# Spreading the softmax reciprocals over 64 partitions: PE transposes against a trip through DRAM

## Chip, cores and metric

The kernel runs on one core of a Trainium2 chip. The metric is the device time of one execution in microseconds (us); lower is better. Before the change the median of three runs was 1174.25 us (1172.53 to 1176.54).

## What is computed

Attention with a memory term, for 4 batches, 8 heads, 576 positions and 64 values a head, followed by two gated feed-forward layers (MoE and MoE2, 2304 rows, width 512, inner width 1536), all in fp32:

```python
scores = scale * np.matmul(q, k.transpose(0, 1, 3, 2))      # causal mask
a = np.exp(scores - scores.max(-1, keepdims=True))
a /= a.sum(-1, keepdims=True) + 1e-09
local = np.matmul(a, v)
mem_out = mem_ret / mem_norm                                # q_p M_prev and q_p z_prev
attn = g * mem_out + (1 - g) * local                        # g = sigmoid(beta)
x = attn as [2304, 512]
x = (sigmoid(x @ w_gate) * (x @ w_val)) @ w_out             # MoE
out = ((x @ w_a) * (x @ w_b)) @ w_out2                      # MoE2
```

## The kernel before, in words

Attention works on 16 pairs (a batch and two of its heads; `p` counts them, 4 pairs make a batch). Rows of a pair lie in five blocks: X_ (blocks 0, 2, 3) and Y_ (blocks 1, 4). In pass `p` of the main loop the scores and exponentials of pair `p` are made, and what is left of pair `p - 1` (`old`) is finished:

- `scores` (L195): q times k in fp32 for both heads into two large PSUM tiles `sc`. `expo` (L224 on DVE, L229 on ACT): minimum, exponential and row sums `sm`.
- `turn_w` (L311): transposes of the exponentials on PE through the identity matrix, into PSUM tiles `tp`, and an evacuation (`aw`, L149 on ACT or L147 on DVE). There are three `tp` buffers (a fourth for the first pairs), and every transpose, every evacuation and every product with v takes one.
- `sums(old)`: the memory norm and the row sums, with the gate folded in, become `t` [128 x 10], one value for each row, block and head; L290 takes its reciprocal on DVE. L292 on POOL copies each value to 64 columns, `rt` [128 x 5 x 2 x 64].
- `turn_r(old, X_)` and `turn_r(old, Y_)`: five transposes of `rt` on PE (L341) into two `tp` tiles and two copies on ACT (L346) into `x` [128 x 576]: now each of a head's 64 partitions holds the reciprocals of all rows.
- `pv(old, ...)`: products with M_prev (L360) and with v (L366), accumulated in a `tp` tile; L372 on DVE multiplies it with `x`, in place, and L376 stores `x` to DRAM.
- Between these the work for the first feed-forward layer is laid in: `M()` issues one group of three matmuls (L471 to L473, written `m<-xs,w` or `m<-gh,w`) at a time, `fill` issues steps of the weight preparation (loads `st`, L388 and L390; DVE L398 to L417; ACT; POOL), and `split_a` turns finished `x` tiles into pairs `xs`. `room(old)` makes sure that the `x` tile of four pairs ago has been split, since there are four of them.

All DMAs are issued by SP, in one order. A scheduler sets the order of each engine's instructions from the order of the program and from its own estimates; PE, DVE, ACT, POOL and SP then each run their list in that order. After the 16 pairs come the rest of the first layer and the second layer (matmuls `gv` and `mo`), which the change does not touch.

Of the kernel before, what the change touches and what calls it, by code (L numbers as in the profile page):

```python
# [9 lines left out]
F32 = mybir.dt.float32  # L10
F32R = mybir.dt.float32r
AF = mybir.ActivationFunctionType
# [7 lines left out]
def kernel(  # L20
# [16 lines left out]
    nc = tc.nc  # L37
    P = 128
    B, H, S, D = q.shape
    NPAIR = H // 2  # L40
# [5 lines left out]
    NB = 5  # L46
    ZX = 320
# [7 lines left out]
    vec, act, pool, pe = nc.vector, nc.scalar, nc.gpsimd, nc.tensor  # L55

    const = ctx.enter_context(tc.tile_pool(name="const", bufs=1))
    dram = ctx.enter_context(tc.tile_pool(name="dram", bufs=1, space=bass.MemoryType.DRAM))
# [6 lines left out]
    xp = lctx.enter_context(tc.tile_pool(name="xp", bufs=4))  # L65
    work = lctx.enter_context(tc.tile_pool(name="work", bufs=2))
    at = rctx.enter_context(tc.tile_pool(name="at", bufs=2, side="right"))
# [8 lines left out]
    H2 = (0, 1)  # L76
# [4 lines left out]
    def rows(i):  # L81
        return P if i else 64

    ident = const.tile([P, P], F32, name="ident")
# [4 lines left out]
    scs = [psa.tile([P, 1024], F32, tag=f"sc{e}", name="sc") for e in H2]  # L89
    sms = [at.tile([P, NB, 2], F32, name=f"sm{i}", bufs=1) for i in H2]  # L90
    xd = [dram.tile([P, NPAIR, S], F32, name=f"xd{i}") for i in range(B)]
    xb = {}
    st = {}

    X_, Y_ = (0, 2, 3), (1, 4)
    AT = {0: 0, 2: 64, 3: 192, 1: 320, 4: 448}
# [3 lines left out]
    def place(p):  # L100
        b, r = divmod(p, NPAIR)
        return b, 2 * r
# [48 lines left out]
    def tp():  # L151

        turns[0] += 1
        return (psx if psm is None and turns[0] % 4 == 0 else pst).tile([P, 512], F32, tag="tp", name="tp")
# [113 lines left out]
    def sums(p):  # L268

        _, h = place(p)
        t = at.tile([P, NB, 2], F32, tag="t", name="t")
        vec.scalar_tensor_tensor(
            out=t, in0=sms[p % 2], scalar=1e-9,
            in1=og[:, h:h + 2].rearrange("p (o h) -> p o h", o=1).to_broadcast([P, NB, 2]),
            op0=ALU.add, op1=ALU.mult,
        )
        nr = st.pop(("nr", p))  # L280
        vec.tensor_tensor(out=nr, in0=nr, in1=t, op=ALU.mult)
        qp = st.pop(("qp", p))
        for a in (slice(0, 3), slice(3, NB)):
            w = a.stop - a.start
            pool.tensor_tensor(
                out=mix(p)[:, a, :, 0:64], in0=qp[:, a],
                in1=nr[:, a].rearrange("p i (h o) -> p i h o", o=1).to_broadcast([P, w, 2, D]),
                op=ALU.mult,
            )
        vec.reciprocal(out=t, in_=t)  # L290
        rt = at.tile([P, NB, 2, D], F32, tag="rt", name="rt", bufs=1)
        pool.tensor_copy(  # L292
            out=rt, in_=t.rearrange("p i (h o) -> p i h o", o=1).to_broadcast([P, NB, 2, D])
        )
        st["rt", p] = rt


    PA = [(2, 1, 0), (3, 1, P), (2, 2, 2 * P), (3, 2, 3 * P)]
# [17 lines left out]
    def turn_mix(p, name):  # L316
# [11 lines left out]
        a = evac("am" + "XY"[name == "Y"], t, c, 1 if name == "Y" else 2, name in EDVE)  # L328
        for m, e in enumerate(es):
            st["m", p, e, blocks] = a[:, m * c // len(es):(m + 1) * c // len(es)]  # L330

    def turn_r(p, blocks):

        b, pr = divmod(p, NPAIR)
        if blocks is X_:
            xb[b, pr] = xp.tile([P, S], F32, tag="x", name="x")
        t0, w = (0, ZX) if blocks is X_ else (ZX, S - ZX)
        r = tp()
        for i in blocks:
            m, c = rows(i), AT[i] - t0  # L340
            pe.transpose(  # L341
                out=r[:, c:c + m],
                in_=st["rt", p][0:m, i].rearrange("p h d -> p (h d)"),
                identity=ident[0:m, 0:m],
            )
        act.activation(out=xb[b, pr][:, t0:t0 + w], in_=r[:, 0:w], func=AF.Copy)  # L346

    def pv(p, blocks):

# [360 lines left out]
    if True:  # L710
        start()
        wst = w_stream(
            [(w1, 0, c, kind, wp) for kind in range(3) for c in range(MA)]
            + [(w1, 0, c, kind, wp if c < KA else None) for c in range(MA, NCH) for kind in range(3)],
            2,
        )
        left = [1 + 9 * KA]

        def w_next():

            if left[0]:
                left[0] -= 1
                next(wst)

        batches = list(range(B - 1))
        cur, deferred, finished, cut_a = [], [], [], []
        split_q = []

        def settle():
            while deferred:  # L730
                deferred.pop(0)()

        def M():

            settle()
            if not cur:
                if not batches:
                    return False
                cur.append(moe_a(batches.pop(0)))
                cur.append(next(cur[0]))  # L740
            b, key, f, after = cur[1]
            if b not in cut_a or key not in ws:
                return False
            with tc.issue_after(st["anchor"].ins):
                f()
            if after:
                deferred.append(after)
            nx = next(cur[0], None)
            if nx is None:
                cur.clear()  # L750
            else:
                cur[1] = nx
            return True

        def Ms(k=1):
            for _ in range(k):
                M()

        def split(k):
            while k and split_q and split_q[0][0] <= done[0] and split_q[0][3] <= len(finished):  # L760
                _, f, a, _ = split_q.pop(0)
                f(*a)
                if a[-1] == KD - 1:
                    cut_a.append(a[0])
                k -= 1

        def fill(p):
            settle()
            split(1)
            if p >= 1:  # L770
                with tc.issue_after(st["pace"].ins):
                    for _ in range(1 if p < 4 else 2):
                        w_next()

        def room(p):

            old = divmod(p - 4, NPAIR)
            while any(x[1] is split_a and x[2] == old for x in split_q):
                split(1)
                if not M():  # L780
                    w_next()

        for b in range(B - 1):
            for kk in range(KD):
                split_q.append((NPAIR * b + kk + 1, split_a, (b, kk), b))
        for kk in range(KD):
            split_q.append((NPAIR * (B - 1) + kk + 1, split_last, (kk,), B - 1))

        load_q(0)
        load_k(0)  # L790
        load_z(0)
        load_v(0)
        for key in "kq":
            turn(0, key)
        turn4(0)
        for p in range(NP + 1):
            new = p < NP
            nx = p + 1 if p + 1 < NP else None
            old = p - 1 if p else None
            if p == NPAIR:  # L800
                pctx.close()
                mctx = ExitStack()
                psm = mctx.enter_context(
                    tc.tile_pool(name="psm", bufs=1, space=bass.MemoryType.PSUM, side="right")
                )

            if nx:
                load_q(nx)
                load_k(nx)
            if new:  # L810
                scores(p, X_)
                expo(p, X_)
            if old is not None:
                for e in H2:
                    turn_w(old, e, "B")
            Ms()
            if old is not None:
                for e in H2:
                    turn_w(old, e, "C")
                sums(old)  # L820
            Ms(2)
            fill(p)
            if new:
                phi1(p)
                if p:
                    load_v(p)
            if nx:
                load_z(nx)
                for key in "kq":
                    turn(nx, key)  # L830
            Ms(2)
            fill(p)

            if new:
                scores(p, Y_)
                expo(p, Y_)
            Ms()
            if old is not None:
                for name in "01Y":
                    turn_mix(old, name)  # L840
            Ms()
            if nx:
                turn4(nx)
            fill(p)
            if new:
                for e in H2:
                    turn_w(p, e, "A")
                phi2(p)
            Ms(2)
            if old is not None:  # L850
                room(old)
                turn_r(old, X_)
                turn_r(old, Y_)
                Ms()
                pv(old, X_)
                pv(old, Y_)
            Ms(2)
            fill(p)
        while cur or batches or split_q or deferred:
            M()  # L860
            fill(NP)
        while left[0]:
            w_next()
# [100 lines left out]
```

## Time and profile before

| | |
|---|---|
| median of 3 runs | 1174.25 us |
| the profiled execution, its own time | 1178.19 us |
| its span, first to last instruction | 1176.4 us (1.8 us lie around it) |
| PE busy | 1138.2 us (97%), mean granted clock 0.984 |
| weight loads of PE | 900.8 us (77%) |
| DVE busy | 542.1 us (46%) |
| ACT busy | 454.6 us (39%) |
| POOL busy | 285.1 us (24%) |
| DMA queue of SP | 24.1% of 16 engines |
| chain that ended last | PE 85%, DVE 7%, ACT 4%, others 4% |

The attention part ends near 369 us of the span; the rest is the feed-forward layers. The shares are means over stages with different limits, so a change in the attention part is read from its own stretch. The granted clock is a share of the full TensorE clock (2.4 GHz); 0.5 is its lower level (1.2 GHz).

### The profile page before, as it was taken

Reading aid. Unit: us, or ns where it says so; the run is one execution under the profiler, and the core shown is the slowest. Engines: PE = TensorE matmul, PEld = TensorE weight load, DVE = VectorE, ACT = ScalarE, POOL = GpSimd, SP = SyncE. Lnnn points to the kernel's source line nnn. Section 1 sums busy time; section 2 is a strip of 40 time slices with the busy share of each in tenths; the row PEclk is TensorE's granted clock in tenths of the full one; section 3 lists DMA queues with packets and bytes.
Section 4 is the critical chain, followed back from the end, with each engine's and each line's share of the span. In section 5 each row is a group of like instructions: output and inputs, shape, how many; then the busy total and the mean of one; then the engine's idle time right before and its main releaser. Section 6 shows DMA issues by size and latency. Waiting matters only on the chain.

```text
span 1176.4 us, 15633 instructions
## 1 busy us (share of the span) xinstructions
PE 1138.2 (97%) x5928; PEld 900.8 (77%) x5928; DVE 542.1 (46%) x1169; ACT 454.6 (39%) x977; POOL 285.1 (24%) x298
## 2 busy tenths in 40 slices
PE   6889889999999999999999999999999999999998
PEld 4555557667677888998788888888888888888897
DVE  5897875554544997127821388861100200200111
ACT  5777655765744444133411243432111211211221
POOL 2675563242230112111111111111111111111111
PEclk9898989999999999999999999999999999999999
DMA  6444434123002434013330334421000200100000
GB/s 155 107 124 123 118 83 122 47 70 105 25 22 98 133 112 135 37 55 126 118 115 1 107 111 159 125 72 36 36 1 1 72 1 1 59 1 1 5 36 19
DMA packets 109563, 84.39 MB, mean 72 GB/s; under 512 B 69168, under 2 KB 96816, under 8 KB 108592
## 3 DMA queue, kind: packets, MB, share of 16 engines
q1 hardware_dynamic: 109488, 83.39, 24.1%
q8 instruction: 47, 0.77, 0.3%
q14 instruction: 28, 0.23, 0.1%
HBM read 66.06 MB, written 17.30 MB: 71 GB/s over the span
## 4 chain that ended last, share of the span: by engine, by line
PE 85%; DVE 7%; ACT 4%; issue 1%; DMA 1%; POOL 1%; SPq 1%; POOLq 0%; DVEq 0%; ACTq 0%
PE gv L472 15%; PE gv L473 15%; PE gv L471 15%; PE mo L670 4%; PE mo L669 4%; PE mo L668 4%; PE mo L471 3%; PE mo L472 3%; PE mo L473 3%; PE sc L195 3%; PE m L471 3%; PE tp L366 3%; PE m L472 2%; PE m L473 2%; PE tp L311 2%; ACT s L229 2%
## 5 line engine op out<-in xcount | busy, mean ns | idle before, releaser
L471 PE MATMUL gv<-xs,w 128*128 128x512 f32 (+1 forms) x864 | 319.3, 370 | 1.3 <-ACT xs L623 1.3
L472 PE MATMUL gv<-xs,w 128*128 128x512 f32 (+1 forms) x864 | 319.2, 369 | 0.4 <-DVE xs L624 0.2
L473 PE MATMUL gv<-xs,w 128*128 128x512 f32 (+1 forms) x864 | 318.9, 369 | 0.0
L558 POOL TENSOR_TENSOR gl<-sg,gh 128x512 fp32r<-128x512 f32 (+1 forms) x120 | 144.8, 1207 | 698.6 <-ACT gh L149 698.6
L552 DVE TENSOR_TENSOR sg<-gv,sg 128x512 f32<-128x512 f32 (+1 forms) x108 | 68.2, 631 | 419.3 <-PE gv L473 414.9
L471 PEld LDWEIGHTS gv<-xs,w 128*128 128x128 f32 x864 | 163.1, 189 | 30.9 <-ACT xs L623 1.5
L472 PEld LDWEIGHTS gv<-xs,w 128*128 128x128 f32 x864 | 163.2, 189 | 30.6 <-DVE xs L616 0.8
L473 PEld LDWEIGHTS gv<-xs,w 128*128 128x128 f32 x864 | 163.2, 189 | 28.9
L149 ACT ACTIVATE gh<-sg 128x512 fp32r<-128x512 f32 (+1 forms) x120 | 70.6, 589 | 221.5 <-DVE sg L552 221.2
L638 ACT ACTIVATE sg<-gv 128x512 f32<-128x512 f32 (+1 forms) x108 | 59.1, 547 | 218.6 <-PE gv L473 216.5
L670 PE MATMUL mo<-w,gl 128*128 128x512 f32 x216 | 85.0, 394 | 0.1
L669 PE MATMUL mo<-w,gh 128*128 128x512 f32 x216 | 84.8, 393 | 0.0
L668 PE MATMUL mo<-w,gh 128*128 128x512 f32 x216 | 84.8, 392 | 0.0
L229 ACT ACTIVATE s<-s,mx 128x320 f32<-128x320 f32 (+3 forms) x128 | 77.5, 608 | 11.9 <-DVE mx L224 11.9
L149 ACT ACTIVATE aw<-tp 128x512 f32<-128x512 f32 (+2 forms) x112 | 56.0, 514 | 53.0 <-PE tp L311 32.8
L399 ACT ACTIVATE wt<-wt,rebias 128x512 int32<-128x512 int32 x72 | 51.8, 720 | 59.1 <-DVE wt L398 58.9
L224 DVE CUSTOM_DVE_ANT_0 s<-sc,mask 64x64 f32<-64x64 f32 (+4 forms) x160 | 69.0, 480 | 10.2 <-PE sc L195 7.8
L471 PE MATMUL mo<-gh,w 128*128 128x512 f32 (+1 forms) x192 | 70.2, 366 | 0.0
L472 PE MATMUL mo<-gl,w 128*128 128x512 f32 (+1 forms) x192 | 70.2, 366 | 0.0
L473 PE MATMUL mo<-gh,w 128*128 128x512 f32 (+1 forms) x192 | 70.2, 366 | 0.0
L195 PE MATMUL sc<-kt,qt 64*128 64x320 f32 (+4 forms) x384 | 63.1, 443 | 0.6 <-DVE mx L224 0.3
L436 ACT ACTIVATE w<-wt 128x512 fp32r<-128x512 f32 x57 | 36.0, 631 | 41.3 <-DVE wt L433 40.5
(102 smaller groups left out, 1593.7 us busy)
## 6 DMA issues: line engine op xcount, KB each, us to landing
st<-in_moe_w_out_dram SPq DMA_DIRECT2D x24, 512.0 KB, 3.5
st<-in_moe_w_gate_dram SPq DMA_DIRECT2D x12, 512.0 KB, 3.6
st<-in_moe_w_val_dram SPq DMA_DIRECT2D x12, 512.0 KB, 3.6
st<-in_moe_w_a_dram SPq DMA_DIRECT2D x12, 512.0 KB, 3.6
st<-in_moe_w_b_dram SPq DMA_DIRECT2D x12, 512.0 KB, 3.7
xd<-x SPq DMA_DIRECT2D x16, 288.0 KB, 2.8
qn<-in_q_dram SPq DMA_DIRECT2D x32, 128.0 KB, 3.0
kn<-in_k_dram SPq DMA_DIRECT2D x32, 128.0 KB, 3.1
```

Source lines behind the costliest of these rows:

```text
L149: act.activation(out=out, in_=src, func=AF.Copy)
L195: st["anchor"] = pe.matmul(scs[e][0:m, SC0[i] + a:SC0[i] + z], lhsT=st["q", p][r, r0:r0 + m], rhs=st["k", p][r, a:z], start=True, stop=True,)
L224: st["pace"] = vec.tensor_tensor_reduce(out=s, in0=scs[e][0:m, SC0[i]:SC0[i] + w], in1=mask[0:m, c:c + w], scale=1.0, scalar=BIG, op0=ALU. ...
L229: act.activation(out=o, in_=s, func=AF.Exp, scale=-1.0, bias=mx[0:m, i:i + 1], accum_out=sms[p % 2][0:m, i:i + 1, e],)
L471: pe.matmul(o, lhsT=w[:, 0, ws_], rhs=xh, start=first, stop=False, skip_group_check=True)
L472: pe.matmul(o, lhsT=w[:, 0, ws_], rhs=xl, start=False, stop=False, skip_group_check=True)
L473: pe.matmul(o, lhsT=w[:, 1, ws_], rhs=xh, start=False, stop=last, skip_group_check=True)
L552: st["gate"] = vec.tensor_tensor(out=s[:, 0:n], in0=vps[:, 0:n], in1=s[:, 0:n], op=ALU.mult)
L558: pool.tensor_tensor(out=gl[:, 0:n], in0=s[:, 0:n], in1=gh[:, 0:n].bitcast(F32), op=ALU.subtract)
L668: pe.matmul(mo[f], lhsT=gh[:, t], rhs=w[:, 0], start=first, stop=False)
L669: pe.matmul(mo[f], lhsT=gh[:, t], rhs=w[:, 1], start=False, stop=False)
L670: pe.matmul(mo[f], lhsT=gl[:, t], rhs=w[:, 0], start=False, stop=c == NCH - 1)
```

## The change

`rt`, its copy on POOL and `turn_r` are gone. In their place `spread(old)` transposes `t` [128 x 10] once on PE (L301 of the new file) into a `tp` tile [10 x 128], ACT copies it to `tt` (L305), SP stores it in five pieces of two rows each to a DRAM tile `rd` [2 x 576] (L310; one of four in turn), and SP loads each row of `rd` back into 64 partitions of `x` (L315, two transfers of 64 x 576). `spread` and the call of `room` stand right behind `sums(old)`, early in the pass, where `turn_r` stood near its end.

```diff
+    rds = [dram.tile([2, S], F32, name=f"rd{i}") for i in range(4)]
...
         vec.reciprocal(out=t, in_=t)
-        rt = at.tile([P, NB, 2, D], F32, tag="rt", name="rt", bufs=1)
-        pool.tensor_copy(
-            out=rt, in_=t.rearrange("p i (h o) -> p i h o", o=1).to_broadcast([P, NB, 2, D])
-        )
-        st["rt", p] = rt
+        st["t", p] = t
+
+    def spread(p):
...
+        b, pr = divmod(p, NPAIR)
+        r = tp()
+        pe.transpose(
+            out=r[0:2 * NB, 0:P], in_=st.pop(("t", p)).rearrange("p i h -> p (i h)"), identity=ident
+        )
+        tt = at.tile([2 * NB, P], F32, tag="tt", name="tt")
+        act.activation(out=tt, in_=r[0:2 * NB, 0:P], func=AF.Copy)
+        rd = rds[p % 4]
+        for i, k in ((0, 1), (1, 1), (2, 2), (4, 1)):
+            for m in range(k):
+                w = rows(i + m)
+                nc.sync.dma_start(
+                    out=rd[:, AT[i + m]:AT[i + m] + w], in_=tt[2 * (i + m):2 * (i + m) + 2, 0:w]
+                )
+        x = xb[b, pr] = xp.tile([P, S], F32, tag="x", name="x")
+        for e in H2:
+            nc.sync.dma_start(out=x[64 * e:64 * e + 64], in_=rd[e:e + 1].broadcast_to([64, S]))
...
-    def turn_r(p, blocks):
-
-        b, pr = divmod(p, NPAIR)
-        if blocks is X_:
-            xb[b, pr] = xp.tile([P, S], F32, tag="x", name="x")
-        t0, w = (0, ZX) if blocks is X_ else (ZX, S - ZX)
-        r = tp()
-        for i in blocks:
-            m, c = rows(i), AT[i] - t0
-            pe.transpose(
-                out=r[:, c:c + m],
-                in_=st["rt", p][0:m, i].rearrange("p h d -> p (h d)"),
-                identity=ident[0:m, 0:m],
-            )
-        act.activation(out=xb[b, pr][:, t0:t0 + w], in_=r[:, 0:w], func=AF.Copy)
...
                 sums(old)
+                room(old)
+                spread(old)
...
             if old is not None:
-                room(old)
-                turn_r(old, X_)
-                turn_r(old, Y_)
                 Ms()
                 pv(old, X_)
                 pv(old, Y_)
```

The scheduler makes a new order from it. Three places of it follow; line numbers of the new file are 1 to 20 off those of the old one (numbers behind names tell buffers apart; L331 is the old L311, L364 the old L360, L370 the old L366, L475 to L477 the old L471 to L473, L196 the old L195, L171 the old L170, L380 the old L376, L108 and L112 the old L107 and L111).

PE, pair 8, from its transposes `tp<-ident,s` to its products with v, before:

```order
L311 MATMUL tp_2364<-ident_87,s_2214 128x128 x4
L473 MATMUL m_2305<-xs_2192,w0_566 128x512
L341 MATMUL tp_2384<-ident_87,rt_2264 128x64
L341 MATMUL tp_2384<-ident_87,rt_2264 128x128 x2
L341 MATMUL tp_2389<-ident_87,rt_2264 128x128 x2
L471 MATMUL m_2379<-xs_1932,w0_743 128x512
L472 MATMUL m_2379<-xs_1932,w0_743 128x512
L473 MATMUL m_2379<-xs_1932,w0_743 128x512
L471 MATMUL m_2379<-xs_2020,w0_743 128x512
L472 MATMUL m_2379<-xs_2020,w0_743 128x512
L473 MATMUL m_2379<-xs_2020,w0_743 128x512
L360 MATMUL tp_2396<-aw_2334,mv_2040 64x320
```

The same place now:

```order
L331 MATMUL tp_2378<-ident_87,s_2218 128x128 x4
L475 MATMUL m_2393<-xs_2084,w0_757 128x512
L476 MATMUL m_2393<-xs_2084,w0_757 128x512
L477 MATMUL m_2393<-xs_2084,w0_757 128x512
L475 MATMUL m_2393<-xs_2196,w0_757 128x512
L476 MATMUL m_2393<-xs_2196,w0_757 128x512
L477 MATMUL m_2393<-xs_2196,w0_757 128x512
L364 MATMUL tp_2400<-aw_2348,mv_2054 64x320
L364 MATMUL tp_2400<-aw_2354,mv_2054 64x320
L370 MATMUL tp_2400<-aw_2140,vn_2053 64x256
```

The three rows of `rt` (five transposes) are gone from between the transposes `tp<-ident,s` and the products; six matmuls of the first layer still stand between.

PE, the same pass, about half a pass earlier, at the scores of the Y_ blocks, now:

```order
L196 MATMUL sc_92<-kt_2066,qt_2073 128x192
L196 MATMUL sc_93<-kt_2066,qt_2073 128x320
L196 MATMUL sc_92<-kt_2066,qt_2073 128x320
L196 MATMUL sc_93<-kt_2066,qt_2073 128x256
L301 MATMUL tp_2268<-ident_87,t_2262 10x128
L196 MATMUL sc_92<-kt_2066,qt_2073 128x256
L171 MATMUL tp_2300<-ident_87,kn_2203 128x128 x4
L171 MATMUL tp_2307<-ident_87,qn_2199 128x128 x4
L475 MATMUL m_2319<-xs_1936,w0_580 128x512
L476 MATMUL m_2319<-xs_1936,w0_580 128x512
L477 MATMUL m_2319<-xs_1936,w0_580 128x512
```

The one new transpose stands inside the scores; from it to the products of pair 8 come 28 transposes of other tiles, 24 matmuls `m` and seven score matmuls.

SP, the trip of pair 8 and its neighbours, now (before, the load of `kn` stood right behind the store `xd`):

```order
L130 DMA mv_2293<-in_v_dram 64x2x64
L132 DMA vn_2292<-in_v_dram 128x4x64 x2
L380 DMA xd1_97<-x_2025 128x576
L310 DMA rd0_100<-tt_2270 2x64
L310 DMA rd0_100<-tt_2270 2x128 x4
L315 DMA x_2277<-rd0_100 64x576 x2
L108 DMA kn_2675<-in_k_dram 128x2x64
```

Seven transfers a pair are new, and the loads wait for the landing of the five stores with SP standing, so what is behind them waits too. In pairs 1, 5 and 6 a load of a weight piece `st` stands between the stores and the loads; the other pairs have none there.

## Rows read from the trace of the kernel before

**Rows 1.** Windows: us, busy of PE, PEld, DVE, ACT, POOL, clock, DMA, GB/s

```profile
30.00:90.00 60.00, 50.45 (x349) 33.46 (x347) 55.12 (x147) 44.66 (x128) 40.77 (x44) 0.91 0.44 118
90.00:180.00 90.00, 79.16 (x468) 53.98 (x467) 68.42 (x161) 57.61 (x135) 50.45 (x51) 0.91 0.41 109
180.00:369.00 189.00, 186.68 (x1201) 133.24 (x1199) 93.13 (x287) 113.39 (x286) 56.78 (x77) 1.00 0.23 65
```

**Rows 2.** Waits of PE, 0 to 180 us: us in total, times, longest

```profile
PE tp L341 <- ACT aw L149: 4.1, 2, 3.3
...
PE tp L341 <- DVE qt L162: 3.2, 3, 2.4
```

**Rows 3.** The tile rt by windows: us, busy of PE, PEld, POOL

```profile
0.00:180.00 180.00, 8.34 (x35) 4.44 (x35) 8.02 (x8) 0.91 0.46 119
180.00:369.00 189.00, 8.20 (x45) 5.16 (x45) 5.77 (x8) 1.00 0.23 65
```

**Rows 4.** Timeline of PE, pair 8: start us, us, line, what

```profile
212.59 0.48 PE L473 MATMUL m<-xs,w 128*128 128x512 f32 x1
213.00 0.86 PE L341 MATMUL tp<-ident,rt 64*128 64x64 f32 x5
213.86 0.50 PE L471 MATMUL m<-xs,w 128*128 128x512 f32 x1
214.20 0.40 PE L472 MATMUL m<-xs,w 128*128 128x512 f32 x1
214.44 0.40 PE L473 MATMUL m<-xs,w 128*128 128x512 f32 x1
```

**Rows 5.** Timeline of PE near 142 us; in brackets, idle before and who ended it

```profile
142.79 0.69 PE L341 MATMUL tp<-ident,rt 128*128 128x128 f32 x2 [3.33 <-ACT aw L149]
```

**Rows 6.** Windows around it, columns as in the first group

```profile
140.00:150.00 10.00, 7.21 (x43) 5.32 (x45) 7.50 (x10) 4.91 (x9) 6.41 (x6) 0.83 0.43 110
165.00:180.00 15.00, 12.58 (x73) 8.48 (x72) 9.31 (x24) 6.71 (x18) 7.20 (x6) 0.77 0.47 119
```

**Rows 7.** Timeline of ACT at the same place

```profile
142.16 0.58 ACT L149 ACTIVATE aw<-tp 128x512 f32<-128x512 f32 x1
```

**Rows 8.** Timeline of DVE: one operation, beside a copy to rt and alone

```profile
113.26 1.06 DVE L243 TENSOR_SCALAR e<-qn 128x640 f32<-128x640 f32 x1
...
214.67 0.49 DVE L243 TENSOR_SCALAR e<-qn 128x640 f32<-128x640 f32 x1
```

**Rows 9.** Timeline of POOL at the first of these

```profile
113.25 0.72 POOL L292 COPY rt<-t 128x640 f32<-128x640 f32 x1
```

**Rows 10.** The tile x: durations in ns, least, median, most

```profile
L346 ACT ACTIVATE x<-tp x32: 363/408/444, 32.4 to 362.4; 128x320 f32<-128x320 f32 x16, 128x256 f32<-128x256 f32 x16
```

**Rows 11.** DMA issues: KB each, median us from issue to landing

```profile
xd<-x SPq DMA_DIRECT2D x16, 288.0 KB, 2.8
...
zb<-in_z_prev_dram SPq DMA_DIRECT2D x16, 64.0 KB, 3.3
...
xt<-xd SPq DMA_DIRECT2D x16, 32.0 KB, 1.9
```

**Rows 12.** Timeline of SP: start us, time to issue

```profile
38.34 0.60 SPq L128 DMA_DIRECT2D mv<-in_M_prev_dram  x1
...
188.38 0.38 SPq L107 DMA_DIRECT2D kn<-in_k_dram  x1
```

**Rows 13.** Timeline of PE, the first use of that kn

```profile
224.75 0.60 PE L170 MATMUL tp<-ident,kn 128*128 128x128 f32 x4
```

**Rows 14.** Timeline of DVE, pair 9: reciprocal, and first product with x

```profile
208.67 0.22 DVE L290 RECIPROCAL t<-t 128x10 f32<-128x10 f32 x1
...
241.90 0.49 DVE L372 TENSOR_TENSOR x<-tp,x 128x320 f32<-128x320 f32 x1 [2.68 <-PE tp L366]
```

**Rows 15.** Waits of SP's queue, 0 to 180 us: us in total, times, longest

```profile
SPq L390 <- DVE wl L412: 36.5, 9, 10.1
SPq L388 <- DVE wl L412: 18.6, 5, 7.3
```

## The prediction

> **What bounds the kernel now.** I read the windows first. The attention part has two regimes [rows 1]. From 30 to 90 us DVE is the fullest engine, 55.1 of 60 us, while PE has 9.6 us of holes; from 90 to 180 us DVE has 68.4 of 90 and PE 79.2. From 180 to 369 us PE is busy 186.7 of 189 us at the full granted clock and nothing else is near full. So in the late stretch a microsecond of PE work taken out is a microsecond of time, and in the early one it may only become a longer hole. Behind 369 us the program is the same. Then I read the tile `rt`, which shows what will be removed, the timeline of PE around one removed group, to see what it really costs there, and the waits, to see whether the removed instructions were themselves late.
>
> **Removed: five transposes a pair.** The tile `rt` keeps PE busy 8.34 us for 35 transposes before 180 us and 8.20 us for 45 behind it [rows 3]. Busy time overlaps in a pipelined engine, so I take the cost from starts: in pair 8 the group begins at 213.00 and the next matmul at 213.86, which is 0.86 us, or 0.17 a transpose [rows 4]. The neighbours pay a little too: from one `m` matmul to the next it is 0.24 us (214.20 to 214.44), but 0.41 from the last one to the group (212.59 to 213.00) and 0.34 behind it (213.86 to 214.20). Those two changes of kind cost 0.27 us more, so the group is worth 0.86 to 1.13 us.
>
> **Added on PE: one transpose a pair.** It has the shape of the removed ones on its output side, so 0.17 us, and 0 to 0.27 us for the change of kind inside the scores. The net is 0.86 - 0.17 = 0.69 us a pair, or 1.13 - 0.44 = 0.69 if both pay their changes; the ends are 0.42 and 0.96 us. I take 0.69. It waits for the reciprocal of the pair, and that is old by then: for pair 9 the reciprocal ends near 208.9 us and the products with `x` begin at 241.9 [rows 14].
>
> Late stretch: 45 transposes are nine pairs, 9 x 0.69 = **6.2 us** (3.8 to 8.6).
>
> **Early stretch: seven pairs.** The PE work is worth 7 x 0.69 = 4.8 us if PE were the limit. The copy to `rt` on POOL goes too, and DVE feels it: the same DVE operation took 1.06 us beside a copy of 0.72 us and 0.49 us alone [rows 8, 9]. The loss of up to 0.57 us doesn't meet each copy; with half of the seven hit it is about 2.0 us of DVE time, in the stretch where DVE is the fullest. That is 6.8 us on two engines that share the limit, and since what one saves the other may hold back, I take half, **3.4 us**. The ends are below nothing (next rivals) and well above.
>
> **ACT and POOL.** ACT loses two copies of 0.41 us a pair [rows 10] and gets one of a 10 x 128 tile, 0.41 us at most; POOL loses 0.7 us. Neither is the limit after 180 us, and I cost both at nothing: PE's list covers them. A `tp` buffer less is taken a pair (two go, one comes), which I count in the rivals alone.
>
> **Added: the trip through DRAM.** No row of before shows such a chain, so I add it from the nearest. Transpose 0.27 us with its changes, ACT copy 0.35 us (at most 0.41), four issues on SP before the fifth store, 0.38 to 0.60 us each [rows 12], so about 1.9 us; the landing of a small transfer counted from its issue, 1.9 us for 32 KB and 2.8 for a store of 288 KB [rows 11], so 2.3; one more issue, 0.4; and the landing of the second broadcast load, 2.8 to 3.3 us [rows 11], so 3.0. That is 8.2 us, between 7.0 and 10.0. It lies beside PE's list: from the new transpose to the products of pair 8 the new order has 24 matmuls `m` of 0.24 us, 5.8 us, and 28 transposes that cost 4.8 us at the 0.17 of a removed one, before a single score. The trip is covered by over 2 us, and I cost it at nothing. If that cover were gone, DVE would stand in front of the product with `x`, holding a `tp` buffer, and PE would follow.
>
> SP stands while the stores land, so what is queued behind it is late by the trip's length, mostly loads of `q` and `k`. They are early by far: the `kn` issued at 188.38 is first used at 224.75 us, 36 us later [rows 12, 13]. The tile `x` is claimed sooner, but its last reader, four pairs back, is long through. Both at nothing.
>
> The Trainium skill speaks against such transfers. "DMA: Bandwidth & Descriptors", section "Rules for kernel authors", says that many small transfers should be joined into a large one, since below 64 KB one pays mostly overhead; the five stores carry 1 KB or less. By that rule the trip is nearly all latency, and fully exposed it would add 16 x 8.2 = 131 us, for 1305 us. The rows agree on the latency, 1.9 us for 32 KB against 2.8 for 288 KB, but the sum above needs only the cover.
>
> **Sum.** 6.2 + 3.4 = 9.6 us off the profiled execution's 1178.19 us, 1168.6 us. That execution lies 3.9 us above the median of the runs, 1174.25 us, and most of a change should carry over, so I forecast 1174.25 - 9.6 = **1164.7 us**. About 0.3%, 3.5 us, is what a measurement of this kernel can tell from no change.
>
> **Rival 1, the early stalls go as well.** PE stood 7.3 us before the removed transposes for a `tp` buffer, 4.1 behind ACT and 3.2 behind DVE [rows 2]. The longest, 3.33 us at 142.79, came from an evacuation that ACT began only at 142.16 [rows 5, 7], with `m` matmuls standing behind. And the clock fell there: 0.83 over 10 us and 0.77 over 15 us around the two longest stalls [rows 6], so 3.4 and 6.9 us at the lower level (1.2 GHz), half of which, 5.1 us, is lost work. Now the matmuls `m` come before the next instruction that needs a buffer. If all of it goes, 7.3 + 5.1 more is won: 1152.3 us. Against it: the products need the same evacuations, so part of the stall only moves. Chance 0.14, mostly in part, near 1158.
>
> **Rival 2, the early saving is eaten.** The products now stand one group closer to the transposes that feed them, and an evacuation takes 0.58 us [rows 7]. In the early pairs, with few or no `m` between, PE then waits for ACT where it used to transpose `rt`: a wait of 0.69 us a pair takes back the 4.8 us of PE work, and the DVE time alone moves nothing. If half of the late gain goes the same way, what is left is 3.1 us: 1171.1 us, no change that can be told. Chance 0.16.
>
> **Rival 3, slower: the trip waits for a weight buffer.** In pairs 1, 5 and 6 SP has a load `st` between the stores and the loads of `x`. Such loads wait on SP for DVE to free their buffer: 14 waits, 55.1 us together, 3.9 us in the mean and 10.1 at the longest [rows 15]. The place is the product with `x` on DVE, behind which DVE's own list stands. The mean adds to 8.2 + 3.9 = 12.1 us, which the 10.6 us of counted PE work and the scores in it just cover; the longest, 18.3 us, is over by 7.7 us at most. With a drop of the clock, 1.7 us lost as at 142 us, that is 9.4 us a pair, 28.2 us in three pairs, and 1174.25 - 9.6 + 28.2 = 1192.9 us. It decides against the change from 9.6 / 3 - 1.7 = 1.5 us of lateness in each of the three. For it: DVE is at its fullest there. Against it: the same fullness stretches DVE's way from the reciprocal to the product too, and a `st` that waits is freed before the product in DVE's own list. Chance 0.12, half of it under 1180, since only one wait in 14 is as long as that.
>
> That the change doesn't do what it says is no case here: the new order shows the five transposes gone in all 16 pairs.
>
> **How the numbers follow.** The forecast has 0.58, rival 1 0.14, rival 2 0.16, rival 3 0.12. The forecast's own range comes from the ends of its terms, 3.8 to 8.6 us late and 0 to 6.8 us early: 1158.9 to 1170.5 us. The range given reaches below it into rival 1, to 1156, and above through rival 2 to the mild end of rival 3, to 1176; outside are the far half of rival 1 and most of rival 3, under 0.2. Faster by over 0.3% (below 1170.7) are the forecast and rival 1, less a little: 0.70; within it rival 2 and the mildest of rival 3: 0.18; slower 0.12.
>
> **What would show it.** Right: behind the same work PE's attention part ends some 9 us before 369, two thirds of it won between pair 7 and pair 15; no wait of DVE's product L376 for the DMA of `x`; in the tile `x` the loads land several microseconds before that product; DVE less busy in the first 180 us. Wrong: PE idle in front of L364 for ACT in the early pairs (rival 2); DVE idle in front of L376 until a DMA, or SP waiting at L315 for long (rival 3); new half-clock stretches behind holes of PE, which none of my terms has.

## The result, and the profile after

The changed kernel takes 1161.66 us (median of four runs, 1160.05 to 1162.84) against 1173.39 us for the kernel before in the same comparison: a ratio of 0.9896 [0.987, 0.9921], some 12 us faster. The forecast was 1164.7 us. A second measurement of the same kernel (e10, four runs) gave 1159.87 us and 0.9891 [0.9877, 0.9904].

The profiled execution took 1162.84 us. The page's span and its busy times:

```profile
span 1160.9 us, 15655 instructions
...
PE 1124.1 (97%) x5864; PEld 891.5 (77%) x5864; DVE 532.8 (46%) x1169; ACT 447.6 (39%) x961; POOL 272.9 (24%) x282
```

PE has 64 instructions fewer than before (5928): 80 transposes gone, 16 new. DVE, ACT and POOL are busy 9.3, 7.0 and 12.2 us less.

The windows of the attention part from 90 us on, columns as in [rows 1]:

```profile
90.00:180.00 90.00, 82.24 (x533) 58.49 (x530) 75.97 (x195) 64.57 (x158) 56.37 (x56) 1.00 0.49 137
180.00:357.00 177.00, 174.20 (x1104) 125.68 (x1103) 86.60 (x259) 103.36 (x251) 43.67 (x60) 1.00 0.28 78
```

The first row is the one to look at. From 90 to 180 us PE now does 533 instructions where it did 468, DVE 195 where it did 161, and the granted clock is 1.00 instead of 0.91 [rows 1]. Much of that contrast belongs to the profiled execution of before: e1 and e8 below, which by their medians are no faster than before and 3 us faster, show 519 and 524 instructions of PE there at 0.98. The late stretch is as full of PE as it was.

The stretches in which the granted clock is 0.5 (half-clock stretches) show where that clock went. After, the three that lie in the attention part, and the rest up to 180 us (us, busy of PE, granted clock, DMA share, GB/s):

```profile
24.30:31.10 6.80, 6.27 (x27) 0.50 0.40 105
48.20:51.60 3.40, 3.13 (x15) 0.50 0.81 233
78.90:85.80 6.90, 6.05 (x22) 0.51 0.47 125
85.80:180.00 94.20, 86.05 (x556) 1.00 0.49 136
```

Before, the same view of its seven such stretches up to 180 us, the last two (us, busy of PE, PEld, DVE, ACT, POOL, then as above):

```profile
142.20:145.60 3.40, 2.81 (x8) 2.33 (x9) 3.37 (x4) 1.70 (x5) 3.26 (x3) 0.51 0.16 37
169.50:176.30 6.80, 6.57 (x31) 3.72 (x33) 3.45 (x8) 3.77 (x8) 2.17 (x3) 0.50 0.68 169
```

All seven are 30.6 us with PE busy for 29.8; the three of after are 17.1 us with 15.5. The profiled execution of before is slower than any of before's runs timed here (1170.62 to 1177.75 us), and its clock, 0.984, was low even for that kernel: over the 48 runs of before in the experiments the mean granted clock is 0.988, over the eight runs of the changed kernel 0.991. So the profiles overstate this part.

Some of PE's waits up to 180 us for ACT and DVE (us in total, times, longest):

```profile
PE tp L344 <- ACT kt L167: 4.3, 4, 1.6
...
PE m L475 <- DVE sg L556: 2.0, 1, 2.0
PE tp L364 <- DVE qt L163: 1.9, 2, 1.5
PE tp L344 <- ACT tt L305: 1.7, 1, 1.7
```

The 7.3 us at the removed transposes [rows 2] are gone, and part of them stands elsewhere: 2.0 us at `m`, 1.9 at the products with M_prev (1.5 there before), 1.7 at a transpose that waits for the new copy `tt`. PE's holes up to 180 us were 30.1 us and are 25.8, as they are in e1, which is no faster than before.

The trip is hidden. DVE's longest wait up to 360 us is for PE, and none of the product's waits is for a DMA; SP's queue waits at its stores for `tt`, and little at the loads:

```profile
DVE x L376 <- PE tp L370: 34.7, 19, 6.3
```

```profile
SPq L310 <- ACT tt L305: 33.2, 12, 4.8
...
SPq L315 <- DMA rd<-tt: 12.4, 14, 2.3
```

Pair 9 on PE and SP (start us, us) shows how the new steps stand:

```profile
211.35 0.28 PE L301 MATMUL tp<-ident,t 128*10 128x128 f32 x1
211.56 0.70 PE L196 MATMUL sc<-kt,qt 64*128 64x256 f32 x2
```

```profile
212.50 1.45 SPq L310 DMA_DIRECT2D rd<-tt  x5
215.04 1.11 SPq L315 DMA_DIRECT2D x<-rd  x2
```

The transpose begins at 211.35, the second load is issued at about 215.6, and the product with `x` begins at 225.47. Over the 16 pairs the first of these ways takes 3.5 to 8.8 us and the second 4.0 to 16.1 us; together they are 10.5 us at the least.

**A budget.** For all runs below I split the profiled span into three: PE's holes (span less PE busy), what PE lost at the lower clock (half of its busy time in half-clock stretches), and the rest, its work at the full clock. For the changed kernel that is 1160.9 - 1124.1 = 36.8 us of holes, 7.7 us lost and 1116.4 us of work. The split is rough by some 3 us: PE's ends are modelled, and of the kernels with the trip those with most booked as lost at the half clock (e4, e5, e6) come out with the least work, so half is too much there. Behind pair 15's last product with `x` all kernels run the same 3807 PE instructions, in 807.3 to 811.2 us, so some 2 us of a single profile's span say nothing of the change.

| profiled execution | span | holes | lost at half clock | work |
|---|---|---|---|---|
| before | 1176.4 | 38.2 | 16.7 | 1121.5 |
| e1, before, turn early | 1168.3 | 36.3 | 10.0 | 1121.9 |
| e8, before, two rt | 1166.7 | 34.7 | 10.2 | 1121.8 |
| after | 1160.9 | 36.8 | 7.7 | 1116.4 |
| e10, after again | 1157.6 | 35.4 | 7.9 | 1114.3 |
| e2, four transposes more | 1165.0 | 35.6 | 10.2 | 1119.2 |
| e5, ACT copies, all at the start | 1164.9 | 36.8 | 16.1 | 1112.0 |
| e5b, two ACT copies more | 1160.4 | 38.7 | 6.8 | 1114.9 |
| e6, one `tp` step more | 1161.1 | 35.9 | 14.2 | 1111.0 |
| e7, two `tp` steps, both | 1170.7 | 36.9 | 11.5 | 1122.3 |
| e11, both in one `tp` | 1171.0 | 45.1 | 9.8 | 1116.1 |
| e3, POOL copy | 1155.7 | 30.7 | 9.8 | 1115.1 |
| e9, POOL copy, two buffers | 1153.2 | 30.8 | 6.6 | 1115.8 |
| e4, spread late | 1182.8 | 59.9 | 14.7 | 1108.2 |

### The profile page after: what moved, and what is told of

Same layout as the page of the kernel before. It is cut to its first block, busy times and chain, and to the rows that moved or that the text cites. A ratio compares the mean times of both kernels' runs of the same rounds, so it can differ in the third digit from the quotient of the medians.

```text
span 1160.9 us, 15655 instructions
## 1 busy us (share of the span) xinstructions
PE 1124.1 (97%) x5864; PEld 891.5 (77%) x5864; DVE 532.8 (46%) x1169; ACT 447.6 (39%) x961; POOL 272.9 (24%) x282
## 3 DMA queue, kind: packets, MB, share of 16 engines
q1 hardware_dynamic: 112368, 88.18, 25.9%
## 4 chain that ended last, share of the span: by engine, by line
PE 68%; DVE 15%; DMA 10%; ACT 4%; issue 2%; SPq 1%; POOL 1%; POOLq 0%; ACTq 0%; DVEq 0%
PE gv L476 11%; PE gv L477 11%; PE gv L475 11%; PE mo L674 4%; PE mo L673 4%; PE mo L672 4%; PE sc L196 3%; PE tp L370 2%; PE m L475 2%; PE m L476 2%; DMA st<-in_moe_w_gate_dram 2%; PE m L477 2%; DMA st<-in_moe_w_a_dram 2%; PE tp L331 2%; DVE w L444 2%
## 5 line engine op out<-in xcount | busy, mean ns | idle before, releaser
L475 PE MATMUL gv<-xs,w 128*128 128x512 f32 (+1 forms) x864 | 318.8, 369 | 2.7 <-ACT xs L627 1.2
L477 PE MATMUL gv<-xs,w 128*128 128x512 f32 (+1 forms) x864 | 318.3, 368 | 0.0
L475 PEld LDWEIGHTS gv<-xs,w 128*128 128x128 f32 x864 | 162.8, 188 | 32.8 <-ACT xs L627 1.4
L477 PEld LDWEIGHTS gv<-xs,w 128*128 128x128 f32 x864 | 162.8, 188 | 28.6
L225 DVE CUSTOM_DVE_ANT_0 s<-sc,mask 128x320 f32<-128x320 f32 (+4 forms) x160 | 69.0, 481 | 28.3 <-PE sc L196 16.2
L196 PE MATMUL sc<-kt,qt 64*128 64x320 f32 (+4 forms) x384 | 69.5, 437 | 1.0 <-DVE mx L225 0.7
L475 PE MATMUL mo<-gh,w 128*128 128x512 f32 (+1 forms) x192 | 70.2, 366 | 0.0
L477 PE MATMUL mo<-gh,w 128*128 128x512 f32 (+1 forms) x192 | 70.2, 366 | 0.0
```

The lines of the kernel that those rows point to most:

```text
L196: st["anchor"] = pe.matmul(scs[e][0:m, SC0[i] + a:SC0[i] + z], lhsT=st["q", p][r, r0:r0 + m], rhs=st["k", p][r, a:z], start=True, stop=True,)
L225: st["pace"] = vec.tensor_tensor_reduce(out=s, in0=scs[e][0:m, SC0[i]:SC0[i] + w], in1=mask[0:m, c:c + w], scale=1.0, scalar=BIG, op0=ALU. ...
L475: pe.matmul(o, lhsT=w[:, 0, ws_], rhs=xh, start=first, stop=False, skip_group_check=True)
L477: pe.matmul(o, lhsT=w[:, 1, ws_], rhs=xh, start=False, stop=last, skip_group_check=True)
```

## The experiments

Each expectation is quoted as it was written before its run and names its theories; ratios are to the kernel before in the same comparison. What is added in e2, e3, e5 to e7, e9 and e11 is read by nothing.

**Is it the place?** e1 is the kernel before with `room` and `turn_r` moved to where `spread` stands:

```diff
                 sums(old)
+                room(old)
+                turn_r(old, X_)
+                turn_r(old, Y_)
...
             if old is not None:
-                room(old)
-                turn_r(old, X_)
-                turn_r(old, Y_)
                 Ms()
```

> The kernel before with one thing moved: room and the two turn_r stand behind sums, where the change has spread; the copy to rt, five transposes and two ACT copies a pair all stay. Theory S (most of the gain comes from the place: late in the pass the transposes stood for a tp buffer with matmuls of the first layer queued behind them, and the clock fell): 1163 to 1168 us, about 60% to 80% of the gain, and full clock from 90 to 180 us. Theory W (it is the PE work taken out, 0.69 us a pair): 1171 to 1175 us, no change.

1172.76 us over 12 runs, 0.9991 [0.9978, 1.0005]. The place alone gives nothing, although it makes quite another order of PE's instructions. At the new place PE waits for the two copies (L346), 10.3 us up to 180 us, where in the changed kernel it waits 3.3 us for `tt`:

```profile
PE tp L324 <- ACT x L346: 6.5, 3, 3.2
...
PE tp L170 <- ACT x L346: 3.8, 2, 2.7
```

e1 also gives the cleanest comparison by stage. Cut at the ends of pair 7's and pair 15's last product with `x`, it has the same PE instructions in each part as the changed kernel, but for 40 transposes of `rt` against 8 of `t`. The first two parts, e1 and then e10 (us, busy of PE, granted clock, DMA share, GB/s):

```profile
0.00:190.51 190.51, 164.69 (x1050) 0.95 0.48 124
190.51:359.80 169.29, 166.73 (x1072) 1.00 0.21 59
```

```profile
0.00:183.32 183.32, 157.40 (x1018) 0.95 0.54 143
183.32:349.29 165.97, 164.11 (x1040) 1.00 0.26 74
```

The change is worth 7.2 us in the first part and 3.3 in the second, and the rest behind them differs by 0.2. PE's holes in the first part are the same, 25.8 and 25.9 us. The profiled execution of e1 is the fastest of its twelve and that of e10 lies at its median, so the sum, 10.7 us, is rather too small.

**Is it PE's work?** e2 gives the changed kernel four transposes a pair back, into the same `tp` tile:

```diff
+        for c in (1, 2, 3, 1):
+            pe.transpose(out=r[:, c * P:c * P + P], in_=ident, identity=ident)
         tt = at.tile([2 * NB, P], F32, tag="tt", name="tt")
```

> The changed kernel with four more 128 x 128 transposes a pair beside its one, of the identity into unused columns of the same tp tile, so that PE has its five back at the early place; no copy on POOL, one on ACT, the trip as it is. Theory W: 16 x 0.69 = 11 us come back if PE is the limit all along, 1168 to 1173 us. Theory S: only the late stretch pays, 9 x 0.69 = 6 us at most and 4 by the traces, 1164 to 1168 us, with the first 180 us as in the changed kernel.

1164.78 us, 0.9924 [0.991, 0.9939]: 0.0033 above the changed kernel, 3.9 us. Its budget agrees, 1119.2 us of work against 1114.3 to 1116.4. By that a third of the gain is this work, less than I booked, though 3.9 us is no more than another order can make (e8 and e3 below).

**The POOL copy.** e3 makes `rt` on POOL again, unused:

```diff
         st["t", p] = t
+        rt = at.tile([P, NB, 2, D], F32, tag="rt", name="rt", bufs=1)
+        pool.tensor_copy(
+            out=rt, in_=t.rearrange("p i (h o) -> p i h o", o=1).to_broadcast([P, NB, 2, D])
+        )
```

> The changed kernel with the copy to rt on POOL put back (its result unused). My term: half of 2.0 us of DVE time in the early stretch, so 1162 to 1164 us; if POOL's copy were the cause of the early gain (DVE is the fullest engine from 30 to 90 us), 1166 us or more.

1157.21 us, 0.9863 [0.9845, 0.9882]: not slower but some 3.5 us faster than the changed kernel, outside both ranges. DVE is busier with the copy, 536.8 us here and 540.3 in e9 against 532.8 and 534.0, but that does not show in the time. e9 says more on it.

**The trip uncovered.** e4 moves `room` and `spread` of the changed kernel to where `turn_r` stood:

```diff
                 sums(old)
-                room(old)
-                spread(old)
...
             if old is not None:
+                room(old)
+                spread(old)
                 Ms()
```

> The changed kernel with room and spread where turn_r stood, right before the products. The trip takes 6 to 7 us by the trace of the changed kernel and finds only the products and the few matmuls before them as cover, 2 to 4 us. If DVE then stands in front of the product with x and PE follows: 3 us or more a pair, 1195 to 1230 us. If DVE's and PE's other work hides it (a tp buffer more is free than before): 1162 to 1172 us.

1185.81 us, 1.0108 [1.0089, 1.0126], some 25 us above the changed kernel and between the two ranges. DVE's longest wait up to 380 us is now the trip's:

```profile
DVE x L376 <- DMA x<-rd: 38.9, 13, 12.4
```

The place, worth nothing to the old way, is what lets the new one be free. PE's holes go to 59.9 us, some 23 more.

**ACT's copies.** e5 adds two copies a pair of the removed widths, from a constant:

```diff
+        dx = at.tile([P, 576], F32, tag="dx", name="dx", bufs=1)
+        act.activation(out=dx[:, 0:320], in_=dm, func=AF.Copy)
+        act.activation(out=dx[:, 320:576], in_=dm[:, 0:256], func=AF.Copy)
```

> The changed kernel with two more ACT copies a pair behind its one, 128 x 320 and 128 x 256, from a constant tile in SBUF, so that ACT has the time of the old evacuations back, with no tp buffer and no transpose. Theory A (ACT's time in the first 180 us is what the change saves, 0.8 us a pair): 1166 to 1171 us. Theory T (it is the tp buffers): 1160 to 1164 us, no change.

1163.11 us, 0.9931 [0.9917, 0.9944], but it doesn't answer the question. Since the copies depend on nothing, the scheduler put all 32 at the start, where ACT then is busy 26.77 of the first 30 us.

e5b copies from a tile of the pair instead, so that each copy stays in its pass:

```diff
+        dx = at.tile([P, S], F32, tag="dx", name="dx", bufs=1)
+        mf = mix(p).rearrange("p i h d -> p (i h d)")
+        act.activation(out=dx[:, 0:320], in_=mf[:, 512:832], func=AF.Copy)
+        act.activation(out=dx[:, 320:576], in_=mf[:, 832:1088], func=AF.Copy)
```

> The changed kernel with two more ACT copies a pair, 128 x 320 and 128 x 256, out of the pair's mix tile in SBUF, so that they can't run before the pair (in e5 they read a constant, and all 32 ran in the first 20 us, where they only delayed the start). No tp buffer and no transpose is added. If ACT's time counts by itself: 1165 to 1169 us, 4 us or more over the changed kernel. If ACT is covered, as I costed it: 1160 to 1163 us.

1162.61 us, 0.9914 [0.9901, 0.9928], 2.7 us above the changed kernel in the same comparison, in the profiles 1.5 up to pair 7's last product and 1.3 from there to pair 15's. ACT's time by itself is a small part at most. The copies are not quite the old ones: they read SBUF and not a `tp` buffer, and in four passes they wait for POOL's `mix`, 4.5 us in all.

**One more turn of a `tp` buffer.** e6 adds a second `tp` tile, one transpose and a small copy:

```diff
+        r2 = tp()
+        pe.transpose(out=r2[:, 0:P], in_=ident, identity=ident)
+        dx = at.tile([2 * NB, P], F32, tag="dx", name="dx", bufs=1)
+        act.activation(out=dx, in_=r2[0:2 * NB, 0:P], func=AF.Copy)
```

> The changed kernel with one more tp buffer taken a pair: one more transpose into it and one more ACT copy of 10 x 128 from it, so that the rotation of the three buffers has two steps again where turn_r had two. Theory T: 1165 to 1170 us. Theory A: at most one short ACT operation and one transpose a pair, 1161 to 1164 us.

1162.02 us, 0.9912 [0.9897, 0.9928], 2.5 us above by the ratios. Its mean granted clock over four runs is 0.987, as low as before's and 0.0046 below the changed kernel's, which of 1172 us would be 5.4 us, and still it costs only this: here a lower mean clock did not cost its whole share.

**All of it back.** e7 adds to the changed kernel about what `turn_r` had: two `tp` tiles with two transposes each and a 256-wide copy out of each. With the one of `spread` that makes five transposes and three `tp` tiles a pair.

```diff
+        dx = at.tile([P, S], F32, tag="dx", name="dx", bufs=1)
+        for t0 in (0, 320):
+            r2 = tp()
+            for c in range(2):
+                pe.transpose(out=r2[:, c * P:c * P + P], in_=ident, identity=ident)
+            act.activation(out=dx[:, t0:t0 + 256], in_=r2[:, 0:256], func=AF.Copy)
```

> The changed kernel with two more tp buffers a pair, two transposes into each and an ACT copy of 128 x 256 out of each: PE has its five transposes, ACT two wide copies, and tp three steps instead of two, all at the early place and nothing waits for rt. If A and T together make the gain: 1170 to 1175 us, as the kernel with turn_r moved. If the dependence on the copy to rt makes it: 1164 to 1168 us, as the kernel with four more transposes.

1173.35 us, 1.0015 [1.0005, 1.0024]: the whole gain is gone. The budget is that of the kernel before: 1122.3 us of work, 36.9 of holes. PE has the same 5928 instructions as e2, yet it is busy 4.4 us longer (1133.8 us) and the work is 3 us more. Here the transposes stand in two groups of their own, in e2 behind one that is there anyway; that this is the reason is not shown.

**Both, in one `tp` tile.** e11 has e2's four transposes and two copies, 320 and 256 wide, out of the tile that is there:

```diff
+        for c in (1, 2, 3, 1):
+            pe.transpose(out=r[:, c * P:c * P + P], in_=ident, identity=ident)
         tt = at.tile([2 * NB, P], F32, tag="tt", name="tt")
         act.activation(out=tt, in_=r[0:2 * NB, 0:P], func=AF.Copy)
+        dx = at.tile([P, S], F32, tag="dx", name="dx", bufs=1)
+        act.activation(out=dx[:, 0:320], in_=r[:, 128:448], func=AF.Copy)
+        act.activation(out=dx[:, 320:576], in_=r[:, 256:512], func=AF.Copy)
```

> The changed kernel with four more transposes into its one tp tile and two more ACT copies (320 and 256 wide) out of it, so that PE and ACT have all their work back and tp has one step a pair, as in the changed kernel, held longer. If the gain is PE's and ACT's time: 1169 to 1174 us, as e7 and e1. If it is the number of tp steps: 1163 to 1167 us, little over e2.

1172.76 us, 1.0004 [0.9995, 1.0013], 12.9 us above the changed kernel, with no further `tp` tile. Transposes alone gave 3.9 and copies alone 2.7; together they give twice their sum. Not all of that need be the two together: in e11 the copies hold the `tp` tile, in e5b they hold none, and copies out of it without the transposes were not tried. And it gets there by another way than e7, by holes: 45.1 us. Nearly all of the 12.9 us lies before pair 7's last product, which ends at 195.6 us against 183.3 in e10. Its window from 90 to 180 us and its longest wait up to there:

```profile
90.00:180.00 90.00, 79.72 (x486) 56.59 (x486) 70.01 (x165) 59.06 (x142) 48.45 (x47) 0.90 0.42 116
```

```profile
PE tp L369 <- DVE qt L163: 6.7, 1, 6.7
```

From 90 to 180 us these are before's numbers again [rows 1]: PE near 79 us, the clock 0.9, DVE near 70.

**How much does an order alone move?** e8 is the kernel before with a second buffer for `rt`, no work changed:

```diff
-        rt = at.tile([P, NB, 2, D], F32, tag="rt", name="rt", bufs=1)
+        rt = at.tile([P, NB, 2, D], F32, tag="rt", name="rt", bufs=2)
```

> The kernel before with two buffers for rt instead of one, so that POOL's copy doesn't wait for the transposes of the pair before and the scheduler may order anew; no work is added or taken. It tells how much a new order alone moves: 1172 to 1176 us if nothing hangs on it; 1165 to 1170 if the wait of POOL (8.7 us in the late stretch by the trace of before) or the order counted.

1168.92 us, 0.9973 [0.9962, 0.9985]: 3.2 us for a buffer and the slightly other order that it makes. POOL's wait is gone in its trace too, so the two are not separated.

e9 is e3 with a second buffer:

```diff
+        rt = at.tile([P, NB, 2, D], F32, tag="rt", name="rt", bufs=2)
```

> The changed kernel with the unused copy to rt on POOL, now with two buffers, so the same work as in e3 in another order. If e3's 4 us came from a lucky order: anywhere from 1157 to 1166 us, not the same as e3. If the copy itself helps, against its cost: 1155 to 1159 us again.

1155.67 us, 0.9857 [0.9843, 0.987]: the fastest kernel of the study, and by the ratios the same as e3. In the traces e3 and e9 run PE, DVE, ACT and POOL in the same order, and another than the changed kernel's; their holes are 30.7 and 30.8 us against 35.4 and 36.8, and their work is the same. So the second buffer made no other order, and the test that was meant, the same work in another order, did not happen. The 4 us come with that order, and the copy costs nothing that shows. That the order alone does it, with no copy, was not tried.

No kernel with something added to the changed one has its order. Of the 5848 PE instructions that all of them share, 77 (e5b), 346 (e2), 359 (e3 and e9), 471 (e11), 721 (e6) and 809 (e7) stand at another place of PE's list, so the price of each has that of its order in it.

e10 is the changed kernel once more, to have it beside e5b, e9 and e11.

> The changed kernel as it is, on the chip and in the rounds of these runs, as the base for their differences: 1159 to 1163 us by every theory.

1159.87 us, 0.9891 [0.9877, 0.9904], as the first time.

## Why the forecast held, and which of its steps did not

The time was 3 us from the forecast and well inside the range. Several of the terms were not right.

- **The late stretch, 6.2 us: oversized.** From pair 7's last product with `x` to pair 15's it took 166.8 us before and takes 166.0, with seven more matmuls `m` in it (1.7 us at 0.24) and six more transposes `tp<-ident,s` (1.0 at 0.17): 3.5 us for eight pairs, 0.44 a pair and not 0.69. Against e1, with nothing to set off, it is 3.3 us, 0.42 a pair. The budget says the same for the whole: 1121.7 us of work in the three kernels with `turn_r`, 1115.4 in the two profiles of the changed one, 6.3 us or 0.39 a pair. What failed is "0.69 if both pay their changes". In late pairs the new transpose takes 0.21 us to the next start, 0.31 instead of 0.22 from the score ahead and 0.32 behind it, about 0.40 us, nearly the 0.44 of that sum; so the removed group gave back about 0.84, its own 0.86 without its neighbours' 0.27. One of the two changes of kind stays: in late pairs an `m` behind the transposes `tp<-ident,s` mostly still takes 0.31 or 0.32 us to the next start and not 0.23. Where the rest of the 0.27 went is open; pair 8 was also one case of nine, whose groups took 0.54 to 1.17 us, 0.82 in the mean. The net is near the low end that I had, 0.42.
- **The early stretch, 3.4 us: undersized.** Most of the gain is there, and not two thirds of it between pair 7 and pair 15 as I wrote: pair 7's last product ends at 184.4 us instead of 201.5 in the profiled executions, of which 2.7 us are the seven matmuls and six transposes not yet done. That profile of before is a slow one. By the medians some 12 us were won, and with about 4 for nine late pairs that leaves about 8, against 3.4. From e1 to e10 it is 7.2 us, with the same holes: 164.7 us of PE busy against 157.4, of which 2.1 are the clock (10.0 us lost at the half clock against 7.9) and some 5 work, by a split that is rough by 3. So it looks as if the 4.8 us of PE work that I halved were paid in full, and the clock, which only rival 1 has, came on top. For all of the kernel the mean granted clock gives a measure of it: (0.9914 - 0.9882) of 1172 us is 3.8 us, an upper bound by e6. The sign "DVE less busy in the first 180 us" did not come, 144.4 us against 141.4, since more is done by then.
- **The DVE term, 2.0 us from the POOL copy: not borne out.** e3 and e9 make the copy and are faster. What DVE loses beside the copy does not show at the end; since their order is another, a small loss could be hidden in it.
- **"ACT and POOL ... I cost both at nothing: PE's list covers them"** held for POOL. For ACT it was too little: the copies alone cost 2.7 us (e5b), early and late, and with the transposes that feed them far more (e11, e7). The sentence "A `tp` buffer less is taken a pair ... which I count in the rivals alone" left what the transposes and the copies do together, by the buffer that they hold, without a term.
- **The trip, 8.2 us and hidden: right.** 3.5 to 8.8 us pass from the transpose to the second load's issue, without its landing (5.2 in my sum), and in no pair did DVE wait for it. e4 shows the price of the lost cover, 25 us or 1.6 a pair. That is far from the 131 us of a trip exposed in full: there DVE waits for the loads in 13 of its products, 38.9 us, and the rest of the trip is still covered. The Trainium skill, "DMA: Bandwidth & Descriptors", section "Rules for kernel authors", says that below 64 KB one pays mostly overhead. The trace agrees as far as it goes: in pair 9, 1.1 us pass from the end of the stores' issue (213.95) to that of the first load (215.04), for stores of 1 KB, against 1.9 us from issue to landing for 32 KB [rows 11]. What it cost here was set by where it stands.
- **Rival 1, the stalls and the clock go too: partly what happened.** The 7.3 us at the removed group went, 5.6 stand at three other lines, and the half-clock stretches behind 86 us are gone. But the reason that I gave, the matmuls `m` before the next instruction that needs a buffer, is not separated from the rest; an early place gives the old way nothing (e1), and e1 has no more holes up to pair 7 than the changed kernel.
- **Rival 2** did not come: PE's waits at L364 in the early pairs, 1.9 us, are for DVE and not for ACT, and 1.5 us stood at that line before. **Rival 3** did not come: no wait of L376 for the loads, in pairs 1, 5 and 6 either.

So the forecast was near the time in part by luck, since two errors met: late work booked at one and a half times its size, and an early relief booked at half or less. What is shown is that the transposes and copies together make the gain: with them at the new place and no trip (e1), or back beside the trip (e7, e11), the time is that of before. How the early relief divides between PE's work, the clock and the `tp` buffers stays open. e7 takes the gain away with before's work and e11 with new holes, and kernels with no work taken out differ by 3 to 4 us (e8, e3), so single terms of 2 to 4 us (e2, e5b, e6) are no more than likely.

## What to carry to other kernels

A step that goes from PE through a PSUM buffer and ACT was worth more here where several engines are near full (7.2 us for eight pairs) than where PE alone is (3.3 us for eight): price the two stretches apart. Price a removed group of transposes by what stands at its place afterwards, since the change of kind on either side may stay. A trip through DRAM replaced such a step with no wait of its reader when it started 10.5 us or more ahead of it; started late, the same trip made this kernel slower than before.

## What was not expected

An unused copy on POOL, 16 times 0.7 us, came with a kernel that is 4 us faster, in both kernels that have it, which share one order of the scheduler's. A second buffer that takes no work away moved 3.2 us. And transposes and copies that cost 3.9 and 2.7 us alone cost 12.9 together, where the copies also hold the `tp` tile: in this kernel, with a scheduler behind the program, small costs of one pass did not add.
